# Letting a second query chunk attend while keys and values are still being projected

## The chip, the cores and the metric

The kernel runs on one core of a Trainium2 chip. The metric is the device time of one execution in microseconds. Executions of one kernel agree within about 0.4%.

The engines are named as in the profile: PE (matrix multiplies), PEld (its weight loads), DVE (vector), ACT (activations: exponentials), POOL, and SP, whose queue issues every data transfer. PSUM is the memory that PE writes to.

## The reference, cut to what matters

Two layers, each made of a linear-attention block A and a softmax-attention block B, over S = 2048 positions, D = 1024 features, 32 heads of 32.

```python
def _B_ref(x, wqkv, wo):                       # A is similar, with a feature map in place of softmax
    q, k, v = split_heads(x @ wqkv)            # [H, S, 32] each
    scores = jnp.einsum("bhqd,bhkd->bhqk", q, k) * (Dh ** -0.5)
    p = _softmax(scores, axis=-1)
    o = jnp.einsum("bhqk,bhkd->bhqd", p, v)
    return merge_heads(o) @ wo

for A, B in two layers:                        # shortened
    x = x + _A_ref(_layernorm(x))
    x = x + _B_ref(_layernorm(x))
```

## The kernel before

Positions are cut into four chunks of 512. For each chunk, `to_b(c)` finishes block A, applies the layernorm and projects the keys and values of block B. These projections are the *background*: groups of eight 128x512 matmuls, each of which ends in one PSUM bank that DVE empties.

Attention is cut into *steps*. A step covers four heads (one of 8 head groups g), 256 queries (one of 2 halves) and two key tiles of 128: scores on PE, two exponentials of 128x1024 on ACT, then values and denominators on PE, summed in the PSUM tile ND. A chunk needs 8 x 2 x 8 = 128 steps; a layer has 512, and so 1024 exponentials.

A softmax without the maximum taken off can be summed over key tiles in any order. Chunk 0 therefore attends early: to the keys of chunk c-1 while chunk c is projected. Its partial sums, numerators and denominators, are kept in SBUF.

```python
LAYOUT = {"wide": (0, 8), "mid": (2, 3), "narrow": (3, 1)}   # PSUM: score tiles, background banks

def together(att, blocks, bg, per):            # one step, then `per` units of background work
    bg = iter(bg)
    for b in blocks:
        for _ in b:                            # issues the scores and exponentials of a step
            got = 0.0
            while got < per:                   # a matmul group yields (4, False) and (4, True)
                u, end = next(bg, (1e9, True))
                got += u
                if end:
                    break
            if len(att.lag) > 1:
                att.finish()                   # values and denominators of the step before
    while att.lag:
        att.finish()
    drain(bg)                                  # what is left runs without attention

# in finish(), when a half has seen all key tiles of the block:
    ndc = T("nd", [P, C], F32)
    # ... ndc = nd (+ acc) ...
    rc = T("rc", [P, QH], F32)
    DVE.reciprocal(out=rc[:], in_=ndc[:, QH:C])
    DVE.tensor_tensor(out=oT[...], in0=ndc[:, 0:QH], in1=rc[:], op=ALU.mult)

# one layer
drain(to_b(0, x))
set_mode("mid")
for c in range(1, NCH):
    together(att, [att.block(qs[0], 4 * c - 4, 4 * c, acc, None, c == 1, False)], to_b(c, x), 8)
set_mode("narrow")
for i in range(NCH):                           # chunk 0's last block, then chunks 1, 2, 3 whole
    # ... work: queries of chunk i+1, then after(i-1): output projection and the next layer's keys
    together(att, [block], chain(*work), 8 if i == 0 else 4)
set_mode("wide")
drain(after(NCH - 1, oT, layer, True))
```

Of the kernel before, what the change touches and what calls it, by code (L numbers as in the profile page):

```python
# [9 lines left out]
ALU = mybir.AluOpType  # L10
AX = mybir.AxisListType
ENG = mybir.EngineType
BF16 = mybir.dt.bfloat16
F32 = mybir.dt.float32
# [18 lines left out]
def kernel(  # L33
# [14 lines left out]
    def ppf(w):  # L48
# [4 lines left out]
    serial = [0]  # L53

    BUFS = dict(
        w=3, c8=3, x=2, q=2, kv=2, st=2, E=6, ea=8, acc=4, f=6, r=3, sq=4, nd=2,
        rc=2, kvm=2, sm=6, rcol=3, nc=3, ab=1, t16=1,
    )

    def T(tag, shape, dt):  # L60
        serial[0] += 1
        return sb.tile(shape, dt, tag=tag, name=f"{tag}_{serial[0]}", bufs=BUFS.get(tag, 1))

    def Dr(name, shape, dt=BF16):
        return dram.tile(shape, dt, tag=name, name=name)
# [18 lines left out]
    xb_d = [Dr(f"xb_d{c}", [P, G, C]) for c in range(NCH)]  # L84
    ra_d = [Dr(f"ra_d{c}", [P, C], F32) for c in range(NCH)]
    rb_d = [Dr(f"rb_d{c}", [P, C], F32) for c in range(NCH)]
    kT_d = Dr("kT_d", [P, G, S])
    v_d = Dr("v_d", [P, G, S // P, P])
    wpq_d = Dr("wpq_d", [P, G, D])
# [386 lines left out]
    class Attention:  # L476
# [1 line left out]
            self.lag = []  # L478
            self.nd = None

        def load_kv(self, k0, k1, g):
            kt = T("kv", [P, 2, S], BF16)
            n = k1 - k0
            SP.dma_start(out=kt[:, 0, 0:n * P], in_=kT_d[:, g, k0 * P:k1 * P])
            SP.dma_start(
                out=kt[:, 1, 0:n * P].rearrange("p (t d) -> p t d", d=P),
                in_=v_d[:, g, k0:k1, :],
            )
            return kt

        def block(self, q, k0, k1, acc, oT, first, last):

            kv = self.load_kv(k0, k1, 0)
            for g in range(G):
                nxt = None
                for half in range(2):
                    for kc in range(0, k1 - k0, 2):
                        self.step(q, kv, g, half, kc, kc == 0, kc + 2 == k1 - k0,
                                  acc, oT, first, last)
                        if nxt is None and g + 1 < G:  # L500
                            nxt = self.load_kv(k0, k1, g + 1)
                        yield
                kv = nxt

        def step(self, q, kv, g, half, kc, begin, end, acc, oT, first, last):
            es, tiles = [], []
            for i in range(2):
                tiles.append(ps_tile(f"S{PS['sring'] % PS['ns']}", 2 * C))
                PS["sring"] += 1
            for k in range(2):  # L510
                for j in range(4):
                    rows = slice(32 * j, 32 * j + 32)
                    o = (j % 2) * C + k * QH
                    PE.matmul(  # L514
                        tiles[j // 2][:, o:o + QH],
                        lhsT=kv[rows, 0, (kc + k) * P:(kc + k + 1) * P],
                        rhs=q[rows, g, half * QH:(half + 1) * QH],
                        start=True, stop=True, tile_position=(32 * j, 0),
                        skip_group_check=True,
                    )  # L520
            for i in range(2):
                e = T("E", [P, 2, 2, QH], BF16)
                SC.activation(  # L523
                    out=e[:], in_=tiles[i][:].rearrange("p (j k q) -> p j k q", k=2, q=QH),
                    func=ACT.Exp, scale=SCALE,
                )
                es.append(e)
            self.lag.append((kv, g, half, kc, begin, end, acc, oT, first, last, es))

        def finish(self):  # L530

            kv, g, half, kc, begin, end, acc, oT, first, last, es = self.lag.pop(0)
            if begin:
                self.nd = ps_tile("ND", C)
            nd = self.nd
            for i in range(2):
                for part in range(2):
                    for j in range(4):
                        rows = slice(32 * j, 32 * j + 32)
                        col = (kc + i) * P + 32 * j  # L540
                        PE.matmul(  # L541
                            nd[rows, part * QH:(part + 1) * QH],
                            lhsT=ones_bf[:, 0:32] if part else kv[:, 1, col:col + 32],
                            rhs=es[j // 2][:, j % 2, i, :],
                            start=(begin and i == 0 and part == 0), stop=(end and i == 1),
                            tile_position=(0, 32 * j), skip_group_check=True,
                        )
            if not end:
                return
            if first and not last:  # L550
                DVE.tensor_copy(out=acc[g][:, half, :], in_=nd[:])
                return
            if not first and not last:
                DVE.tensor_tensor(
                    out=acc[g][:, half, :], in0=nd[:], in1=acc[g][:, half, :], op=ALU.add
                )
                return
            ndc = T("nd", [P, C], F32)
            if first:
                DVE.tensor_copy(out=ndc[:], in_=nd[:])  # L560
            else:
                DVE.tensor_tensor(out=ndc[:], in0=nd[:], in1=acc[g][:, half, :], op=ALU.add)  # L562
            rc = T("rc", [P, QH], F32)
            DVE.reciprocal(out=rc[:], in_=ndc[:, QH:C])
            DVE.tensor_tensor(
                out=oT[:, g, half * QH:(half + 1) * QH], in0=ndc[:, 0:QH], in1=rc[:],
                op=ALU.mult,
            )

    def drain(gen):  # L570
        for _ in gen:
            pass

    def together(att, blocks, bg, per):


        bg = iter(bg)
        for b in blocks:
            for _ in b:
                got = 0.0  # L580
                while got < per:
                    u, end = next(bg, (1e9, True))
                    got += u
                    if end:
                        break
                if len(att.lag) > 1:
                    att.finish()
        while att.lag:
            att.finish()
        drain(bg)  # L590
# [19 lines left out]
    def chain(*gens):  # L610
        for g in gens:
            yield from g

    def run():
# [41 lines left out]

        for layer in range(2):
            drain(kv_finish())
            acc = [T(f"acc{g}", [P, 2, C], F32) for g in range(G)]
            x = load_x(0)  # L660

            def to_b(c, x):
                res = {}
                sl = Slabs(["pq", "ao", "bk", "bv"] + (["bq"] if c == 0 else []))
                yield from aq_gen(c, x, sl, res)
                yield from bkv_gen(c, res, sl)
                if c == 0:
                    qs[0] = T("q", [P, G, C], BF16)
                    yield from bq_gen(qs[0], res["xc"], res["rstd"], sl)
                else:  # L670
                    SP.dma_start(out=xb_d[c][:], in_=res["xc"][:])
                    SP.dma_start(out=rb_d[c][:], in_=res["rstd"][:])

            qs = {}
            drain(to_b(0, x))
            set_mode("mid")
            oT = None
            for c in range(1, NCH):
                x = load_x(c)
                together(  # L680
                    att, [att.block(qs[0], 4 * c - 4, 4 * c, acc, None, c == 1, False)],
                    to_b(c, x), 8,
                )
            set_mode("narrow")
            oT = T("c8", [P, G, C], BF16)
            for i in range(NCH):
                work = []
                if i + 1 < NCH:
                    qs[i + 1] = T("q", [P, G, C], BF16)
                    work.append(next_q(i + 1, qs[i + 1]))  # L690
                if i:
                    prev = oT
                    oT = T("c8", [P, G, C], BF16)
                    work.append(after(i - 1, prev, layer))
                block = (
                    att.block(qs[i], 0, S // P, None, oT, True, True) if i
                    else att.block(qs[0], 12, 16, acc, oT, False, True)
                )
                together(att, [block], chain(*work), 8 if i == 0 else 4)
            set_mode("wide")  # L700
            drain(after(NCH - 1, oT, layer, True))


    def setup():
# [21 lines left out]
                    in_=i4[:, s, 4 * g:4 * g + 4].unsqueeze(2).to_broadcast([P, 4, DH]),  # L726
                )

    phi = const("phi", [P, G, P])

    def fold_phi(base, dst):

# [38 lines left out]
    def load_x(c):  # L771
        x = T("x", [P, G, C], BF16)
        SP.dma_start(out=x[:], in_=x_d[c][:])
        return x
# [45 lines left out]
```

## Time and profile before

| | us |
|---|---|
| time, median of 2 runs | 3168.32 (3166.51 to 3170.12) |
| span of the profiled run | 3168.3 |
| PE busy, ACT busy | 81%, 67% of the span |

The page of the kernel before: busy time of the engines, then PE and ACT in 40 equal slices of the span, each digit the busy share in tenths.

```profile
PE 2578.0 (81%) x30208; PEld 1123.8 (35%) x30208; DVE 1276.4 (40%) x1931; ACT 2129.9 (67%) x2433; POOL 95.7 (3%) x88
## 2 busy tenths in 40 slices
PE   4886977888888788878878787878788878878877
...
ACT  2441353535498998898896217262629999999996
```

No engine is full. ACT swings: in each layer three hills with valleys between them (the 6th to 11th digit and the 25th to 30th), then a plateau at 8 or 9. A hill is a projection stage with its 32 steps, a valley the rest of that stage.

The busy time by windows: the stretch and its length, then busy us (and instructions) of PE, PEld, DVE, ACT and POOL, the granted PE clock, the share of DMA engines busy and GB/s. The first two stretches are the chunk-2 stage with and without attention; the third is chunk 0's last block; the fourth is 59 us of attention alone.

```profile
core 0: us, PE busy (x) PEld busy (x) DVE busy (x) ACT busy (x) POOL busy (x), PEclk, DMA share, GB/s
519.20:611.50 92.30, 71.14 (x854) 27.85 (x854) 40.43 (x57) 69.84 (x80) 0.00 (x0) 0.82 0.20 63
611.50:672.30 60.80, 53.29 (x243) 23.46 (x243) 27.60 (x45) 1.36 (x4) 0.00 (x0) 0.89 0.57 189
826.60:894.90 68.30, 57.01 (x833) 25.60 (x834) 48.40 (x54) 59.62 (x65) 0.34 (x2) 1.00 0.35 114
1105.00:1164.00 59.00, 45.90 (x762) 20.46 (x760) 11.47 (x12) 59.00 (x65) 0.00 (x0) 1.00 0.11 37
```

- **Attention alone:** ACT is busy 59.00 of 59 us, and its steps start 1.83 us apart: bound by ACT.
- **The chunk-2 stage:** 92 us with attention (not ACT bound: 69.84 busy), then 61 us in which ACT has 1.36 us of work. That second stretch is the drain at the end of `together`.

A part of the timeline, in chunk 0's last block (start, length, engine, line, operation; tiles written <- read). It shows one step with a whole background group. Line 514 is scores, 158 a background group.

```profile
start us, us, engine line op out<-in xcount [idle before <-releaser]
...
831.56 0.28 PE L514 MATMUL S_1283_7422<-q_2540,kv_7343 32*128 32x256 bf16 x2
...
831.89 1.90 PE L158 MATMUL BG_1287_7436<-c_1272_7363,w_7367 128*128 128x512 bf16 x8
...
834.27 0.28 PE L514 MATMUL S_1290_7467<-q_2540,kv_7343 32*128 32x256 bf16 x2
...
835.15 1.75 DVE L564 RECIPROCAL rc_7464<-nd_7462 128x256 f32<-128x256 f32 x1
...
837.28 0.68 DVE L472 TENSOR_TENSOR q_7342<-BG_1294_7481,r_7364 128x512 bf16<-128x512 f32 x1
```

From scores to scores (831.56 to 834.27) is 2.71 us, all of it PE: 0.33 scores, 1.83 background, 0.55 values (which follow the group at 833.72). A step with a whole group is PE bound.

Step times in this text are the spacing of the first exponentials of successive steps. A stage is counted from its first exponential to that of the next stage.

### The profile page before, as it was taken

To read this page: it belongs to the slowest core of one execution; us is meant where nothing else is said; L and a number is where in the kernel's file an instruction comes from. 1 tells how busy PE (TensorE), PEld (TensorE's weight loads), DVE (VectorE), ACT (ScalarE), POOL (GpSimd) and SP (SyncE) were. 2 spreads that over 40 slices of the span, in tenths; PEclk is the share of its full clock that TensorE was granted. 3 is DMA by queue.
4 is the path that set the end of the run, shared out by engine and by line. 5 is a ranking of instruction groups with operands and counts; after the bars stand their busy time and mean duration, and the time that the engine had idled before them with its cause. 6 is when DMAs were issued, how large, how long until landed. Compare 5 with 4: busy or idle time off the path is not lost.

```text
span 3168.3 us, 68293 instructions
## 1 busy us (share of the span) xinstructions
PE 2578.0 (81%) x30208; PEld 1123.8 (35%) x30208; DVE 1276.4 (40%) x1931; ACT 2129.9 (67%) x2433; POOL 95.7 (3%) x88
## 2 busy tenths in 40 slices
PE   4886977888888788878878787878788878878877
PEld 2442433333433333333333332323233333333333
DVE  2566344444544423523522744444446312322222
ACT  2441353535498998898896217262629999999996
POOL 0320000000000100100100100000000000000000
PEclk8897978887999998999999897879799999999999
DMA  7553505152523113212212251515162211211110
GB/s 191 182 156 122 168 28 193 47 173 69 175 88 127 61 48 111 81 42 98 81 41 93 74 183 47 187 34 189 31 212 87 86 58 42 91 58 41 55 42 15
DMA packets 235241, 309.61 MB, mean 98 GB/s; under 512 B 43456, under 2 KB 207296, under 8 KB 227264
## 3 DMA queue, kind: packets, MB, share of 16 engines
q1 hardware_dynamic: 234944, 305.24, 29.4%
q8 instruction: 236, 3.87, 0.5%
q14 instruction: 61, 0.50, 0.0%
HBM read 236.52 MB, written 60.29 MB: 94 GB/s over the span
## 4 chain that ended last, share of the span: by engine, by line
PE 47%; ACT 28%; DVE 14%; issue 6%; DMA 3%; SPq 1%; ACTq 0%; DVEq 0%; POOLq 0%
SPq L766 1%; DMA v_d<-st_5681 0%; DMA v_d<-st_24626 0%; DMA v_d<-st_4111 0%; DMA w_506<-wpk_d 0%; DMA w_1992<-wpq_d 0%; DMA w_245<-in_A_wqkv_dram 0%; DMA w_10216<-wpk_d 0%; DMA wpk_d<-st_492 0%; PE ND_14215 L541 0%; SPq L737 0%; DVE c_2904_18189 L175 0%; DVE c_2317_14246 L175 0%; DVE c_3634_22833 L175 0%; DVE c_3907_24490 L175 0%
## 5 line engine op out<-in xcount | busy, mean ns | idle before, releaser
L541 PEld LDWEIGHTS <-ones 128*32 128x32 bf16 x8192 | 275.6, 99 | 5.9
L188 PEld LDWEIGHTS <-ones 128*128 128x128 bf16 x128 | 12.7, 101 | 113.0 <-issue 111.6
L193 ACT ACTIVATE f_2352<-BG_432_2319,eps 128x512 f32<-128x512 f32 x1 | 0.7, 687 | 52.1 <-PE BG_432_2319 L188 52.1
L193 ACT ACTIVATE f_22867<-BG_3635_22834,eps 128x512 f32<-128x512 f32 x1 | 0.7, 687 | 50.7 <-PE BG_3635_22834 L188 50.7
L403 PEld LDWEIGHTS <-Rsel 128*128 128x128 bf16 x128 | 13.2, 103 | 59.4 <-issue 58.2
L523 ACT ACTIVATE E_23157<-S_3685_23147 128x1024 bf16<-128x1024 f32 x1 | 1.0, 1026 | 46.1 <-PE S_3686_23148 L514 46.1
L523 ACT ACTIVATE E_2642<-S_482_2632 128x1024 bf16<-128x1024 f32 x1 | 1.0, 1024 | 46.0 <-PE S_483_2633 L514 46.0
L158 PEld LDWEIGHTS <-c_5_187 128*128 128x128 bf16 x128 | 13.4, 106 | 43.3 <-DMA w_506<-wpk_d 22.3
L523 ACT ACTIVATE E_27871<-S_4470_27861 128x1024 bf16<-128x1024 f32 x1 | 1.0, 1024 | 33.5 <-PE S_4471_27862 L514 33.5
L523 ACT ACTIVATE E_7356<-S_1267_7346 128x1024 bf16<-128x1024 f32 x1 | 1.0, 1024 | 33.0 <-PE S_1268_7347 L514 33.0
L523 ACT ACTIVATE E_24727<-S_3946_24717 128x1024 bf16<-128x1024 f32 x1 | 1.0, 1024 | 32.7 <-PE S_3947_24718 L514 32.7
L523 ACT ACTIVATE E_26297<-S_4207_26287 128x1024 bf16<-128x1024 f32 x1 | 1.0, 1024 | 32.5 <-PE S_4208_26288 L514 32.5
L523 ACT ACTIVATE E_5782<-S_1004_5772 128x1024 bf16<-128x1024 f32 x1 | 1.0, 1025 | 31.9 <-PE S_1005_5773 L514 31.9
L523 ACT ACTIVATE E_4212<-S_743_4202 128x1024 bf16<-128x1024 f32 x1 | 1.0, 1025 | 31.4 <-PE S_744_4203 L514 31.4
L158 PE MATMUL BG_77_510<-w_506,c_5_187 128*128 128x512 bf16 x8 | 3.3, 592 | 22.0 <-DMA w_506<-wpk_d 22.0
L158 PEld LDWEIGHTS <-ones 128*128 128x128 bf16 x128 | 12.1, 98 | 24.6 <-issue 10.8
L193 ACT ACTIVATE f_24524<-BG_3908_24491,eps 128x512 f32<-128x512 f32 x1 | 0.7, 687 | 29.1 <-PE BG_3908_24491 L188 29.1
L242 POOL MEMSET acc_1680_9926<- 128x16 bf16 x1 | 0.2, 168 | 631.0 <-DVE nd_7851 L562 631.0
L193 ACT ACTIVATE f_27664<-BG_4430_27631,eps 128x512 f32<-128x512 f32 x1 | 0.7, 687 | 27.5 <-PE BG_4430_27631 L188 27.5
L193 ACT ACTIVATE f_4009<-BG_705_3976,eps 128x512 f32<-128x512 f32 x1 | 0.7, 687 | 27.5 <-PE BG_705_3976 L188 27.5
L193 ACT ACTIVATE f_5579<-BG_966_5546,eps 128x512 f32<-128x512 f32 x1 | 0.7, 687 | 27.5 <-PE BG_966_5546 L188 27.5
L193 ACT ACTIVATE f_7149<-BG_1227_7116,eps 128x512 f32<-128x512 f32 x1 | 0.7, 687 | 27.5 <-PE BG_1227_7116 L188 27.5
(12148 smaller groups left out, 9593.7 us busy)
## 6 DMA issues: line engine op xcount, KB each, us to landing
w_245<-in_A_wqkv_dram SPq DMA_DIRECT2D x1, 1024.0 KB, 5.4
w_247<-in_A_wqkv_dram SPq DMA_DIRECT2D x1, 1024.0 KB, 8.5
xa_d_73<-c_5_187 SPq DMA_DIRECT2D x1, 1024.0 KB, 10.3
x_d_69<-x_167 SPq DMA_DIRECT2D x1, 1024.0 KB, 4.4
x_d_70<-x_234 SPq DMA_DIRECT2D x1, 1024.0 KB, 6.5
xa_d_74<-c_37_346 SPq DMA_DIRECT2D x1, 1024.0 KB, 4.2
x_d_71<-x_704 SPq DMA_DIRECT2D x1, 1024.0 KB, 4.7
x_d_72<-x_1090 SPq DMA_DIRECT2D x1, 1024.0 KB, 5.4
```

Source lines behind the costliest of these rows:

```text
L158: PE.matmul(ps, lhsT=lhsT(po), rhs=rhs(po), start=(po == 0), stop=(po == G - 1))
L188: PE.matmul(ps, lhsT=ones_bf[:], rhs=sq[:], start=(po == 0), stop=(po == G - 1))
L193: SC.activation(out=lnv[:], in_=ps, func=ACT.Ln, scale=1.0 / D, bias=eps_t[:])
L242: POOL.memset(v[:, :, :, P:P + 1], 1.0)
L403: PE.matmul(ps, lhsT=Rsel[:, g, s, :], rhs=ab[:], start=True, stop=True)
L523: SC.activation(out=e[:], in_=tiles[i][:].rearrange("p (j k q) -> p j k q", k=2, q=QH), func=ACT.Exp, scale=SCALE,)
L541: PE.matmul(nd[rows, part * QH:(part + 1) * QH], lhsT=ones_bf[:, 0:32] if part else kv[:, 1, col:col + 32], rhs=es[j // 2][:, j % 2, i, :] ...
L766: SP.dma_start_transpose(out=x[:, po, :], in_=A_x[0, c * C:(c + 1) * C, po * P:(po + 1) * P])
```

## The change

The intent is to give ACT work in the valleys. Chunk 1 attends early too: to keys 0 to 1023 during the chunk-2 stage, and to the next 512 during the chunk-3 stage. Both stages move to the narrow layout (three score tiles, one background bank). Room for a second set of partial sums is made by keeping only numerators in SBUF. Denominators, which are equal in the 32 rows of a head, go to DRAM as one row a head, and come back by a broadcast load. The pacing rule in `together` changes as well: in the middle layout a step may now take two group ends, so two of the short broadcast items.

The core of the diff (the rest passes the new arguments along, lets `load_x` run inside `to_b`, and finds room: five `f` tiles instead of six, `phi` in a shared buffer):

```diff
+    den_d = [Dr(f"den_d{i}", [G, 4, 2, QH], F32) for i in range(2)]
@@ load(), called for the next head group
+            dn = T("dn", [P, 2, QH], F32)
+            for j in range(4):
+                SP.dma_start(
+                    out=dn[32 * j:32 * j + 32, :, :],
+                    in_=den_d[acc[1]][g:g + 1, j, :, :].to_broadcast([DH, 2, QH]),
+                )
@@ finish(), block not the last
+                    DVE.tensor_tensor(out=a, in0=num, in1=a, op=ALU.add)
+                    DVE.tensor_tensor(
+                        out=dt[:, half, :], in0=den, in1=dn[:, half, :], op=ALU.add
+                    )
+                if half == 1:
+                    for j in range(4):
+                        SP.dma_start(
+                            out=den_d[acc[1]][g:g + 1, j, :, :], in_=dt[32 * j:32 * j + 1, :, :]
+                        )
@@ together()
-                while got < per:
+                while got < per and ends < max(1, PS["nb"] - 1):
                     u, end = next(bg, (1e9, True))
                     got += u
-                    if end:
-                        break
+                    ends += end
@@ one layer
             set_mode("mid")
-            # chunk 0 attends to keys of chunk c-1 beside to_b(c), c = 1, 2, 3
+            together(att, [att.block(qs[0], 0, 4, acc[0], None, True, False)], to_b(1), 8)
             set_mode("narrow")
+            together(
+                att,
+                [att.block(qs[0], 4, 8, acc[0], None, False, False),
+                 att.block(qs[1], 0, 8, acc[1], None, True, False)],
+                to_b(2), 8,
+            )
+            together(
+                att,
+                [att.block(qs[0], 8, 12, acc[0], None, False, False),
+                 att.block(qs[1], 8, 12, acc[1], None, False, False)],
+                to_b(3), 8,
+            )
+            together(att, [att.block(qs[0], 12, 16, acc[0], oT[0], False, True)], (), 4)
+            # i = 1: att.block(qs[1], 12, 16, ...) with next_q(2) and after(0), 8 a step, then drained
+            # i = 2, 3: as before
```

(Two comments stand for longer lines.) The tiles `dn` and `dt` have one buffer each.

More of the change, by code (lines that the diff above doesn't have):

```diff
@@ L55 @@
     BUFS = dict(
-        w=3, c8=3, x=2, q=2, kv=2, st=2, E=6, ea=8, acc=4, f=6, r=3, sq=4, nd=2,
+        w=3, c8=3, x=2, q=2, kv=2, st=2, E=6, ea=8, acc=4, f=5, r=3, sq=4, nd=2,
         rc=2, kvm=2, sm=6, rcol=3, nc=3, ab=1, t16=1,
@@ L479, in __init__, with load @@
             self.nd = None
-        def load_kv(self, k0, k1, g):
+        def load(self, k0, k1, g, acc, first):
             kt = T("kv", [P, 2, S], BF16)
@@ L488, in load_kv @@
             )
-            return kt
+            if first:
+                return kt, None
+            dn = T("dn", [P, 2, QH], F32)
[4 more added lines that the diff above has]
+                )
+            return kt, dn
         def block(self, q, k0, k1, acc, oT, first, last):
-            kv = self.load_kv(k0, k1, 0)
+            kv = self.load(k0, k1, 0, acc, first)
             for g in range(G):
@@ L500, in block @@
                         if nxt is None and g + 1 < G:
-                            nxt = self.load_kv(k0, k1, g + 1)
+                            nxt = self.load(k0, k1, g + 1, acc, first)
                         yield
@@ L505, in step @@
         def step(self, q, kv, g, half, kc, begin, end, acc, oT, first, last):
+            kv, dn = kv
             es, tiles = [], []
@@ L527, in step @@
                 es.append(e)
-            self.lag.append((kv, g, half, kc, begin, end, acc, oT, first, last, es))
+            self.lag.append((kv, dn, g, half, kc, begin, end, acc, oT, first, last, es))
         def finish(self):
-            kv, g, half, kc, begin, end, acc, oT, first, last, es = self.lag.pop(0)
+            kv, dn, g, half, kc, begin, end, acc, oT, first, last, es = self.lag.pop(0)
             if begin:
@@ L549, in finish @@
                 return
-            if first and not last:
-                DVE.tensor_copy(out=acc[g][:, half, :], in_=nd[:])
-                return
-            if not first and not last:
-                DVE.tensor_tensor(
-                    out=acc[g][:, half, :], in0=nd[:], in1=acc[g][:, half, :], op=ALU.add
-                )
+            num, den = nd[:, 0:QH], nd[:, QH:C]
+            if not last:
+                a = acc[0][g][:, acc[1], half, :]
+                if half == 0:
+                    self.dt = T("dt", [P, 2, QH], F32)
+                dt = self.dt
+                if first:
+                    DVE.tensor_copy(out=a, in_=num)
+                    DVE.tensor_copy(out=dt[:, half, :], in_=den)
+                else:
+                    DVE.tensor_tensor(out=a, in0=num, in1=a, op=ALU.add)
[7 more added lines that the diff above has]
+                        )
                 return
@@ L561, in finish @@
             else:
-                DVE.tensor_tensor(out=ndc[:], in0=nd[:], in1=acc[g][:, half, :], op=ALU.add)
+                DVE.tensor_tensor(
+                    out=ndc[:, 0:QH], in0=num, in1=acc[0][g][:, acc[1], half, :], op=ALU.add
+                )
+                DVE.tensor_tensor(out=ndc[:, QH:C], in0=den, in1=dn[:, half, :], op=ALU.add)
             rc = T("rc", [P, QH], F32)
@@ L579, in together @@
             for _ in b:
-                got = 0.0
-                while got < per:
+                got, ends = 0.0, 0
+                while got < per and ends < max(1, PS["nb"] - 1):
                     u, end = next(bg, (1e9, True))
                     got += u
-                    if end:
-                        break
+                    ends += end
                 if len(att.lag) > 1:
@@ L658, in run, with to_b @@
             drain(kv_finish())
-            acc = [T(f"acc{g}", [P, 2, C], F32) for g in range(G)]
-            x = load_x(0)
-            def to_b(c, x):
+            tiles = [T(f"acc{g}", [P, 2, 2, QH], F32) for g in range(G)]
+            acc = [(tiles, 0), (tiles, 1)]
+            qs = {}
+            saved = {}
+            def to_b(c):
+                x = load_x(c)
                 res = {}
-                sl = Slabs(["pq", "ao", "bk", "bv"] + (["bq"] if c == 0 else []))
+                sl = Slabs(["pq", "ao", "bk", "bv"] + (["bq"] if c < 2 else []))
                 yield from aq_gen(c, x, sl, res)
                 yield from bkv_gen(c, res, sl)
-                if c == 0:
-                    qs[0] = T("q", [P, G, C], BF16)
-                    yield from bq_gen(qs[0], res["xc"], res["rstd"], sl)
+                if c < 2:
+                    qs[c] = T("q", [P, G, C], BF16)
+                    yield from bq_gen(qs[c], res["xc"], res["rstd"], sl)
                 else:
@@ L672, in to_b @@
                     SP.dma_start(out=rb_d[c][:], in_=res["rstd"][:])
-            qs = {}
-            drain(to_b(0, x))
+            drain(to_b(0))
             set_mode("mid")
-            oT = None
-            for c in range(1, NCH):
-                x = load_x(c)
-                together(
-                    att, [att.block(qs[0], 4 * c - 4, 4 * c, acc, None, c == 1, False)],
-                    to_b(c, x), 8,
-                )
-            set_mode("narrow")
-            oT = T("c8", [P, G, C], BF16)
-            for i in range(NCH):
+            together(att, [att.block(qs[0], 0, 4, acc[0], None, True, False)], to_b(1), 8)
+            set_mode("narrow")
+            together(
[9 more added lines that the diff above has]
+                to_b(3), 8,
+            )
+            oT = [T("c8", [P, G, C], BF16)]
+            together(att, [att.block(qs[0], 12, 16, acc[0], oT[0], False, True)], (), 4)
+            for i in range(1, NCH):
+                oT.append(T("c8", [P, G, C], BF16))
                 work = []
@@ L690, in run @@
                     work.append(next_q(i + 1, qs[i + 1]))
-                if i:
-                    prev = oT
-                    oT = T("c8", [P, G, C], BF16)
-                    work.append(after(i - 1, prev, layer))
+                work.append(after(i - 1, oT[i - 1], layer))
                 block = (
-                    att.block(qs[i], 0, S // P, None, oT, True, True) if i
-                    else att.block(qs[0], 12, 16, acc, oT, False, True)
+                    att.block(qs[i], 0, S // P, None, oT[i], True, True) if i > 1
+                    else att.block(qs[1], 12, 16, acc[1], oT[1], False, True)
                 )
-                together(att, [block], chain(*work), 8 if i == 0 else 4)
+                together(att, [block], chain(*work), 4 if i > 1 else 8)
             set_mode("wide")
-            drain(after(NCH - 1, oT, layer, True))
+            drain(after(NCH - 1, oT[-1], layer, True))
     def setup():
@@ L727, in setup @@
                 )
-    phi = const("phi", [P, G, P])
+    phi = T("t16", [P, G, P], BF16)
     def fold_phi(base, dst):
```

## The prediction

> **What bounds the kernel now.** The span is 3168 us, no engine full: PE busy 81%, ACT 67% (the busy table). Each layer's attention is 512 steps of two 128x1024 exponentials. I cut it into blocks of 32 steps by the exponentials' start times (the view of one source line).
>
> - Attention alone, narrow PSUM layout: 58.9 us a block, 1.83 a step, ACT 40 of 40 us busy (windows): ACT bound.
> - With half a background group (four 128x512 matmuls) a step: 1.85 us, nearly free.
> - With a whole group of eight: 2.71 us, PE bound (timeline: scores 0.33, group 1.83, values 0.55).
> - Projection stages of chunks 1-3 (152.6 us each): 92 us with 32 steps, then 60 us in which ACT idles (windows: 2 of 40 us busy) and PE drains some 30 groups at 1.73 us and a 14 us layernorm. Within the 92 us: query groups 3.0 us a step, an 11.5 us wait for DVE's denominator chain, 22 broadcast steps at 2.4-2.5 us, as the middle layout has two score buffers.
>
> **What the change moves.** No work disappears. Chunk 1's first 12 key tiles (96 of its 128 steps) move under the projections of chunks 2 and 3, in the narrow layout. Estimates from these durations, per layer:
>
> | stage | us |
> |---|---|
> | chunk-1 projection, 32 steps; drained tail gains 8 query groups | 152 |
> | chunk-2 projection, 96 steps: query groups 24, denominator 14, broadcasts 25x1.9=48, whole-group steps 24x2.75=66, layernorm 17, pure steps 60 | 229 |
> | chunk-3 projection, 64 steps | 171 |
> | chunk 0's last block, alone | 59 |
> | chunk 1's last block, whole groups, tail drained | 125 (layer 2: 91) |
> | sum | 736 (702) |
> | now, same work | 797 (768) |
>
> Gain 61 + 66 = 127 us. Two removed drains and faster broadcast steps give some 145 us a layer; overlapped whole groups (+0.9 us each over a pure step), two overlapped layernorms (+10 us each) and chunk 0's results projected under 32, not 128 steps take over half back.
>
> **What it adds.** Per layer 160 broadcast loads and 160 stores of denominators on the SP queue, both tiles single-buffered. Key/value loads take 0.3-0.4 us to issue and at least 2.0 us to land (DMA view), as the Trainium skill has it ("DMA: Bandwidth & Descriptors", Anatomy of one DMA: about 2 us fixed). Per head group: 2+4+4 issues, about 4 us; the store tile is free about 5 us after the sum, wanted after 3.7 in pure steps, 5.4 in whole-group steps; part is hidden. Worse behind 1 MB weight loads (5-6 us). Estimate 10, perhaps 30 us a layer. Two half-width DVE operations for one (0.42 against 0.69): free.
>
> 3168 - 127 + 20 gives about **3065 us**, range **3015 to 3115**. Faster by over 2%: 0.80; within 2%: 0.17; slower: 0.03.
>
> **What would show it.** ACT idle in one drain per layer, after chunk 1's projection; chunk-2 and chunk-3 stages near 230 and 170 us without drained tails; broadcast steps near 1.9 us; whole-group steps near 2.75; DVE waits for denominator transfers of about 1 us, not 3; chunk 1's last stage 125/91 us; later stages unchanged.
>
> **What would make it wrong.** DVE waiting several us a head group on the single denominator buffers, holding the value accumulator and background buffer and so PE; SP delaying weight and key loads; the single background buffer stalling projections.

## The result, and the profile after

The changed kernel took 3075.91 us (2 runs, 3073.64 to 3078.18) against 3168.32 us: ratio 0.9708, 95% interval 0.9667 to 0.975. A ratio here is the mean time of one kernel's runs over that of the other's of the same rounds, so not quite the ratio of the medians. The changed kernel, unedited, ran again as a control (below): 3074.9 us, ratio 0.9699. The forecast of 3065 was 11 us low, inside its range.

The page of the changed kernel, the lines that answer to those of before:

```profile
PE 2471.7 (80%) x29928; PEld 1095.4 (36%) x30208; DVE 1330.2 (43%) x2219; ACT 2136.7 (70%) x2433; POOL 95.7 (3%) x88
## 2 busy tenths in 40 slices
PE   4786879798787778878877787978878887878877
...
ACT  2441263769868558898897306277986877999996
```

PE and ACT do nearly the same work in a shorter span. (Some 280 matmul records are missing from this trace, so its lower PE time says nothing.) ACT's first valley of each layer is still there; the two that followed are mostly filled.

The busy time by windows for layer 1, same columns. In order: chunk-1 stage with attention, its drain; chunk-2 stage with background, its pure steps; chunk-3 stage; chunk 0's last block; chunk 1's last block with attention, its drain.

```profile
368.30:469.10 100.80, 78.10 (x907) 32.05 (x920) 55.60 (x98) 69.39 (x81) 0.00 (x0) 0.91 0.29 98
469.10:516.80 47.70, 46.42 (x237) 22.05 (x242) 18.16 (x28) 1.93 (x3) 0.00 (x0) 0.94 0.59 182
516.80:686.80 170.00, 143.66 (x1801) 61.48 (x1825) 73.92 (x131) 128.75 (x144) 0.00 (x0) 0.92 0.39 127
686.80:748.50 61.70, 48.32 (x806) 21.37 (x807) 6.41 (x18) 60.64 (x67) 0.00 (x0) 1.00 0.17 53
748.50:921.80 173.30, 145.58 (x1841) 62.46 (x1865) 80.48 (x151) 130.57 (x147) 0.00 (x0) 0.91 0.40 127
921.80:983.80 62.00, 46.48 (x766) 20.15 (x767) 44.49 (x61) 59.16 (x64) 0.00 (x0) 0.86 0.32 98
983.80:1095.00 111.20, 87.54 (x959) 37.60 (x973) 74.88 (x114) 64.46 (x71) 3.26 (x4) 0.92 0.44 145
1095.00:1130.10 35.10, 20.24 (x108) 8.69 (x108) 24.45 (x35) 7.55 (x13) 8.95 (x8) 0.62 0.28 90
```

The 61 us drain is gone from the chunk-2 and chunk-3 stages; one of 48 us stays after chunk 1's projection, and there is a new one of 35 us at the end, in which ACT has 7.55 us of work and the granted clock is 0.62.

Stage by stage, us. "Forecast" is the table of the prediction, which left out its 10 us a layer for denominators:

| stage | forecast | layer 1 | layer 2 |
|---|---|---|---|
| chunk-1 projection | 152 | 148.5 | 148.4 |
| chunk-2 projection, 96 steps | 229 | 231.8 | 231.7 |
| chunk-3 projection, 64 steps | 171 | 173.3 | 173.2 |
| chunk 0's last block | 59 | 62.0 | 62.4 |
| chunk 1's last block | 125 / 91 | 146.3 | 97.7 |
| sum | 736 / 702 | 761.9 | 713.4 |
| same work before | 797 / 768 | 798.4 | 772.9 |

The stages give 36.5 + 59.5 = 96.0 us, and the spans differ by 3168.3 - 3071.8 = 96.5: the whole difference lies here. The later stages are as before (chunk 2: 270.2 and 243.0 us against 272.5 and 242.0).

Broadcast steps take 1.81 to 1.84 us in the new chunk-2 stage where nothing waits (mostly 2.39 to 2.5 before), whole-group steps 2.71 to 2.73. The denominators do show. A part of the timeline in that stage (SPq lines are transfers being issued; x4 is four of them; L571 adds denominators, L494 loads them, L576 stores them, L551 is values):

```profile
566.28 0.42 DVE L571 TENSOR_TENSOR dt_5023<-ND_5043,dn_4747 128x256 f32<-128x256 f32 x1
...
566.75 3.04 SPq L494 DMA_DIRECT2D dn_4925<-den_d_89  x4
...
569.83 1.16 SPq L576 DMA_DIRECT2D den_d_89<-dt_5023  x4
...
572.29 0.42 DVE L571 TENSOR_TENSOR dt_5175<-ND_5125,dn_4925 128x256 f32<-128x256 f32 x1 [2.27 <-DMA den_d_89<-dt_5023]
...
572.77 0.29 PE L551 MATMUL ND_5195<-E_5152,kv_4922 128*32 128x256 bf16 x2 [2.19 <-DVE dt_5175 L571]
...
573.82 1.02 ACT L533 ACTIVATE E_5222<-S_915_5212 128x1024 bf16<-128x1024 f32 x1 [1.26 <-PE S_916_5213 L524]
```

The sum in `dt` was ready to be stored at 566.7. SP was then in the four loads of the next `dn`, from 566.75 to 569.8, and got to the stores at 569.83. DVE wanted `dt` again at 570.0 and waited 2.27 us. The label names the stores, but the next sum also reads the `dn` of the four loads: by the semaphore updates in the trace the last load landed at 571.38, the last store at 571.88, so only the last 0.5 us is the stores' alone. PE waited behind DVE, and ACT had nothing to do for 1.26 us. The Trainium skill ("DMA: Bandwidth & Descriptors", Anatomy of one DMA) says that a semaphore wait happens on the issuing sequencer before dispatch. This trace agrees: just before, SP issued nothing from 562.5 to 565.8, where its next load waited for PE. The 3.1 us by which the ready stores were late are issue time in one queue: the four loads took 3.04 us there (one of them 1.50; the trace does not show why), and none of the semaphores that the last three wait for changes in that time. Over the trace there are 45 DVE waits for such transfers, 44 us in all (21 in layer 1, 23 in layer 2).

### The profile page after: what moved, and what is told of

Read it like the earlier page. It is cut to its first block, busy times and chain, and to the rows that moved or that the text cites. A ratio compares the mean times of both kernels' runs of the same rounds, so it can differ in the third digit from the quotient of the medians.

```text
span 3071.8 us, 69543 instructions
## 1 busy us (share of the span) xinstructions
PE 2471.7 (80%) x29928; PEld 1095.4 (36%) x30208; DVE 1330.2 (43%) x2219; ACT 2136.7 (70%) x2433; POOL 95.7 (3%) x88
## 4 chain that ended last, share of the span: by engine, by line
PE 48%; ACT 20%; DVE 18%; DMA 5%; issue 5%; SPq 4%; DVEq 0%; ACTq 0%; POOLq 0%
SPq L494 2%; SPq L797 1%; SPq L576 0%; DVE c_1965_11955 L590 0%; DMA w_12339<-in_B_wo_dram 0%; SPq L486 0%; DMA w_1994<-wpq_d 0%; DMA w_508<-wpk_d 0%; DMA w_33472<-in_B_wo_dram 0%; DMA w_247<-in_A_wqkv_dram 0%; DVE c_5294_33088 L590 0%; SPq L768 0%; DVE c_4036_25094 L176 0%; DVE x_12337 L433 0%; DVE x_33470 L433 0%
## 5 line engine op out<-in xcount | busy, mean ns | idle before, releaser
L551 PEld LDWEIGHTS <-ones 128*32 128x32 bf16 x8192 | 270.3, 99 | 5.4
L159 PEld LDWEIGHTS <-c_6_189 128*128 128x128 bf16 x128 | 13.4, 106 | 42.9 <-DMA w_508<-wpk_d 21.5
L159 PEld LDWEIGHTS <-c_2104_12760 128*128 128x128 bf16 x128 | 13.8, 110 | 33.9 <-issue 26.1
L159 PEld LDWEIGHTS <-ones 128*128 128x128 bf16 x128 | 11.8, 98 | 25.1 <-issue 12.5
L159 PE MATMUL BG_78_512<-w_508,c_6_189 128*128 128x512 bf16 x7 | 3.2, 608 | 21.4 <-DMA w_508<-wpk_d 21.2
L159 PEld LDWEIGHTS <-c_3603_22690 128*128 128x128 bf16 x128 | 12.8, 101 | 15.9 <-issue 1.9
L159 PEld LDWEIGHTS <-c_3031_18809 128*128 128x128 bf16 x128 | 10.5, 98 | 20.6 <-issue 13.3
L159 PEld LDWEIGHTS <-c_205_1204 128*128 128x128 bf16 x128 | 12.5, 98 | 14.6
L159 PEld LDWEIGHTS <-c_2444_14866 128*128 128x128 bf16 x128 | 10.4, 97 | 20.1 <-issue 12.5
L159 PEld LDWEIGHTS <-c_133_818 128*128 128x128 bf16 x128 | 12.4, 98 | 14.4
L159 PEld LDWEIGHTS <-c_38_348 128*128 128x128 bf16 x128 | 12.4, 98 | 14.4
L159 PE MATMUL BG_365_1998<-c_361_1990,w_1994 128*128 128x512 bf16 x7 | 3.4, 630 | 11.5 <-DMA w_1994<-wpq_d 11.3
```

Of the source, the lines that this page charges most:

```text
L159: PE.matmul(ps, lhsT=lhsT(po), rhs=rhs(po), start=(po == 0), stop=(po == G - 1))
L551: PE.matmul(nd[rows, part * QH:(part + 1) * QH], lhsT=ones_bf[:, 0:32] if part else kv[:, 1, col:col + 32], rhs=es[j // 2][:, j % 2, i, :] ...
```

## The experiments

Theory: time falls because attention fills the drains, and this pays only in the narrow layout, where a step without a group takes 1.83 us; the denominators give some 10 us a layer back. Rivals: the layout alone did it; the pacing rule is immaterial; the denominators are free, or all of their waits count.

Runs of one call shared a chip; the medians of the kernel before over the four calls were 3168.2, 3170.3, 3168.6 and 3165.6 us. Intervals are 95%.

### The layout alone, on the kernel before

```diff
-            set_mode("mid")
+            set_mode("narrow")
```

> The kernel before with only the PSUM layout of the three projection stages changed from middle to narrow; nothing moved. Theory (the gain is the moved attention; the layout alone shortens 22 broadcast steps by 0.55 us, -12 us a stage, but costs about 0.9 us for each of 24 drained groups, +22 us): about 8 us a stage slower, 3168 to 3240. Rival (the layout is what made the changed kernel faster): 3080 to 3110.

Measured: 3229.06 us, ratio 1.0191 (1.0176 to 1.0206). Layer 1's three stages took 164.1, 162.8 and 164.7 us against 152.5, 153.1 and 154.3; the time from the last attention step of a stage to the next stage grew from 62 to 64 us to 87 to 89. Broadcast steps did fall to 1.81 us. The rival falls: with nothing moved, the single background bank costs more in the drain than the third score tile gains.

### The moved attention in the old layout

```diff
             together(att, [att.block(qs[0], 0, 4, ...)], to_b(1), 8)
-            set_mode("narrow")
             # chunk-2 and chunk-3 stages
+            set_mode("narrow")
             oT = [T("c8", [P, G, C], BF16)]
```

> The changed kernel with the chunk-2 and chunk-3 stages kept in the middle layout (two score buffers, three background buffers). Theory (moved attention pays only where a pure step takes 1.83 us; in the middle layout some 59 steps a layer without a group take 2.4, part offset by two broadcasts a step): about 37 us a layer slower, 3150 (3130 to 3170). Rival (where attention runs is everything, the layout is immaterial): 3060 to 3090.

Measured: 3188.97 us, ratio 1.0067 (1.0052 to 1.0082), slower than the kernel before, and 114 us above the control's median. The direction is the theory's; the size is not, 57 us a layer instead of 37. Layer 1's chunk-2 stage took 271.5 us against 231.8. Up to its last background group it was shorter, 150.6 against 168.2, as two broadcasts share a step. Then 48 steps without a group took 120.9 us, where the changed kernel has 34 in 63.6. The window of those 48 steps and, from the timeline, one step of them (L524 is scores):

```profile
663.10:784.00 120.90, 94.02 (x1169) 36.87 (x1162) 9.63 (x26) 93.02 (x96) 0.00 (x0) 0.53 0.12 39
```

```profile
699.85 0.61 PE L524 MATMUL S<-q,kv 32*128 32x256 bf16 x6 [0.52 <-ACT E L533]
...
700.36 1.94 ACT L533 ACTIVATE E<-S 128x1024 bf16<-128x1024 f32 x2 [0.56 <-PE S L524]
```

With two score tiles, PE waits for ACT to leave a tile (0.52 us), then ACT waits for PE to fill it (0.56 us): 2.50 us a step, and the granted clock is 0.53. It fell from 1.00 to 0.50 at 669.3; the first two of these steps, before that, took 2.39 us, so most of the loss against 1.83 is there at the full clock. Neither half of the change is worth anything without the other.

### The old pacing rule

```diff
-                while got < per and ends < max(1, PS["nb"] - 1):
+                while got < per and ends < 1:
```

> The changed kernel with the old pacing rule (a step takes background work up to the first end of a group, so one broadcast a step in the middle layout). It acts in the chunk-1 stage alone. Theory (that stage stays at 148 us in spite of 8 more query groups because two broadcasts now share a step, which brings the output projection under attention): that stage goes back to before's 152.6 plus 14 for the query groups, 166 us, so 35 us slower over two layers, about 3111 (3100 to 3120). Rival (the pacing rule is immaterial, the drained tail is hidden either way): 3068 to 3084.

Measured: 3111.31 us, ratio 0.9818 (0.9801 to 0.9836); control below. The chunk-1 stage took 167.5 and 168.1 us, 20 more a layer. So 36 us of the change's gain (3111.3 - 3074.9) hang on this small line: broadcasts take 11 steps instead of 22 or more, and the output projection gets under attention before the steps run out. The other 57 us (3168.3 - 3111.3) are there without it.

One rival stays untested: the line alone in the kernel before. That kernel has three middle-layout stages a layer, whose 32 steps take the same 90 us as in this run's chunk-1 stage. If each gained the 20 us measured here, it would be some 120 us in two layers, more than the whole change. This is an estimate from one stage; no run shows it.

### Control

> The changed kernel itself, unedited, as the yardstick for the other runs on this chip: 3076 within 8 us.

Measured: 3074.9 us, ratio 0.9699 (0.9677 to 0.9721).

### No denominator transfers

Loads and stores are taken out; a constant tile is added instead. The result is wrong on purpose.

```diff
-            dn = T("dn", [P, 2, QH], F32)
-            # four broadcast loads
-            return kt, dn
+            return kt, (None if first else den_c)
@@ finish()
-                if half == 1:
-                    # four stores
```

> Wrong result on purpose: no denominator loads or stores, the partial sums add a constant tile instead; same DVE and PE work. In the trace of the changed kernel DVE waits 21 us in layer 1 and 23 us in layer 2 for these transfers. Theory (part of it reaches the critical path, as predicted 10 us a layer, 12 by the long steps I count): 24 us faster than the changed kernel, about 3052. Rival A (hidden entirely): within 5 us of it, 3071 to 3081. Rival B (every wait counts): 44 us faster, about 3032.

Measured: 3057.14 us, ratio 0.9648 (0.9626 to 0.967), below the control's interval. By medians 18 us, by ratios (the runs are of different calls) 16: 8 or 9 a layer, less than half of the 44 us that DVE waits. In the traces of this run and the changed kernel, the chunk-2 and chunk-3 stages and chunk 0's last block are shorter by 4.9, 2.7 and 2.1 us in layer 1, and 1.9, 2.3 and 1.8 in layer 2. Both rivals fall.

### Loads alone taken out, and two outgoing tiles

First, two tiles for outgoing denominators; the buffers fill SBUF, so one `f` tile goes.

```diff
-        nd=2, f=5,   # shortened
+        nd=2, f=4, dt=2,
```

> The changed kernel with two tiles for outgoing denominators (room made by four instead of five f tiles of the same size). In the control's trace 20 of 28 DVE waits for denominator transfers in layer 1 end with a store. Theory (the single outgoing tile is most of the 19 us that the transfers cost): 8 to 14 us faster, about 3064; chunk-2 and chunk-3 stages 2 to 3 us shorter each. Rival (the waits move to the incoming tile, also single, behind the same SP queue): within 4 us of 3075.

Second, the loads alone out, the stores kept; the result is wrong.

```diff
-            dn = T("dn", [P, 2, QH], F32)
-            # four broadcast loads
-            return kt, dn
+            return kt, (None if first else den_c)
```

> Wrong result on purpose: the denominators are stored as in the changed kernel but not loaded back; a constant tile is added instead, as in the run without any denominator transfers (3057, ratio to before 0.9648). Theory (the loads, behind which the SP queue holds the stores, carry most of the 19 us; two outgoing tiles gave only 4): about as fast as the run without any transfer, ratio 0.964 to 0.966, 3055 to 3061. Rival (the stores carry it): ratio 0.968 to 0.970, 3067 to 3075.

Measured: with two tiles, 3070.59 us, ratio 0.9694 (0.9681 to 0.9708), not to be told from the control; the 8 to 14 us did not come. In its trace DVE still waits 16.1 and 21.9 us a layer for these transfers (control 21.9 and 25.1). The count in the expectation was wrong, too: the control's trace has 20 such waits in layer 1, 12 labelled as stores and 8 as loads; in the changed kernel's first trace 10 of 22 are labelled as loads. The label names only what came last, so it was no ground to choose the tile by: a sum waits for the loads of `dn` as well, and in the step shown above they landed 0.5 us before the stores. That is about all that a second outgoing tile could save there. With the loads gone, 3060.70 us, ratio 0.9669 (0.9654 to 0.9684): by the ratio between the two expectations, by the time at the end of the theory's. Of the ratio's 0.0051 between control and no transfers, the loads carry 0.0030 by the mean values, but the interval overlaps both, so the share is rough. How the rest splits between stores, the SP queue and the short `f` ring stays open.

### Half a group a step in the chunk-2 stage

```diff
-                to_b(2), 8,
+                to_b(2), 4,
```

> The changed kernel with half a background group a step in the chunk-2 stage, whose 96 steps then hold all of its background work by my count of the generator's yields (96), in place of 63 steps with whole groups and 33 pure ones. Theory (a whole-group step is PE bound at 2.71 us, a half-group step is ACT bound at 1.85 as in the trace of before): 24 groups x 0.85 us = 20 us a layer faster, about 3036 (3020 to 3050). Rival (that stage is held by denominator transfers and DVE, not by how groups are spread): within 10 us of 3076.

Measured: 3028.54 us, ratio 0.956 (0.9545 to 0.9576). The stage took 207.6 and 208.6 us, 24 and 23 less. Its window in layer 1:

```profile
514.80:722.40 207.60, 179.59 (x2633) 73.99 (x2632) 81.48 (x149) 187.08 (x211) 0.00 (x0) 0.94 0.35 114
```

ACT is busy 187 of 208 us; the steps with half a group take 1.85 to 1.87 us, as read in the trace of before. Whole groups and pure steps side by side were the waste: 2.71 + 1.83 = 4.54 us for a pair that can take 3.70.

### The reciprocal moved to ACT

```diff
-            DVE.reciprocal(out=rc[:], in_=ndc[:, QH:C])
+            SC.activation(out=rc[:], in_=ndc[:, QH:C], func=ACT.Ln)
+            SC.activation(out=rc[:], in_=rc[:], func=ACT.Exp, scale=-1.0)
```

This asks why every second step of chunk 1's last block takes 3.47 us. The changed kernel's timeline there (L159 is a background group, L433 empties its bank, L589 the reciprocal):

```profile
1011.81 1.90 PE L159 MATMUL BG_2043_12389<-c_1772_10818,w_12339 128*128 128x512 bf16 x8
...
1012.43 1.75 DVE L589 RECIPROCAL rc_12372<-nd_12369 128x256 f32<-128x256 f32 x1
...
1014.56 0.68 DVE L433 TENSOR_TENSOR x_12337<-BG_2043_12389,x_12337 128x512 bf16<-128x512 f32 x1
...
1015.29 1.02 PE L159 MATMUL BG_2049_12430<-c_1772_10818,w_12339 128*128 128x512 bf16 x3 [0.70 <-DVE x_12337 L433]
```

The group is done at 1013.7, but DVE is in the reciprocal and the product and empties the bank at 1014.56; the next group starts at 1015.29 after 0.70 us of waiting.

> The changed kernel with the reciprocal of the denominators moved from DVE (1.75 us, 128x256) to ACT as exp(-ln x), two activations of an estimated 0.5 us each. Theory (in chunk 1's last stage every second whole-group step takes 3.47 instead of 2.71 us because the reciprocal delays the background eviction on DVE): these steps fall to about 2.75, the stage is 10 to 12 us shorter a layer; in chunk 2's and 3's stages the ACT time added (1 us an end, 16 ends each) about cancels what the steps of 3.4 us gain. 3050 to 3080 in all; the stage time decides. Rival (these long steps come from the accumulator or the denominator loads): the 3.47 us steps stay.

Measured: 3107.57 us, ratio 0.9807 (0.9789 to 0.9824): worse as a whole. By the expectation the stage time decides, and it fell from the control's 147.6 to 135.7 us in layer 1; a pair of steps fell from 6.18 (3.47 + 2.71) to 5.48 (3.67 + 1.81). In layer 2 it fell by 2.5 us only. So the reciprocal is the cause of the long steps. The guess that the added ACT time cancels in chunk 2's stage held in layer 1 (269.9 us against the control's 270.4) and not in layer 2 (250.7 against 242.0), and it left out chunk 0's last block: where ACT is the bound, two activations of 0.42 us are paid in full (77.2 us against 64.0).

### The drained tail carried on

With the half groups above. `together` returns what is left instead of draining it, and chunk 2's stage takes it first.

```diff
+        if carry:
+            return bg
         while att.lag:
             att.finish()
@@ i = 1, 2, 3
-                work = []
+                work = [rest]
-                together(att, [block], chain(*work), 4 if i > 1 else 8)
+                rest = together(att, [block], chain(*work), 4 if i > 1 else 8, i == 1) or ()
```

> The changed kernel with half a group a step in the chunk-2 stage (measured alone before: 47 us faster) and with chunk 1's last stage not drained: what is left of its background work is carried into chunk 2's stage, which had over 50 pure steps. Theory (chunk 1's last stage took 146 and 98 us, not my 125 and 91, mostly because the drained tail with one background buffer took 35 us, not 22): the stage falls to about 112 and 83 us, chunk 2's stage grows by 10 and 3 us; together with the half groups 3076 - 47 - 36 = about 2993 (2980 to 3010). Rival (the carried work costs in chunk 2's stage what the drain cost): 3020 to 3035.

Measured: 2998.31 us, ratio 0.9461 (0.9444 to 0.9478). Chunk 1's last block took 118.4 and 83.6 us, chunk 2's stage 281.2 and 242.7 (with half groups alone: 147.0 and 97.9, then 269.9 and 243.0). The tail was idle time for the most part: 29 us went and 11 came back in layer 1; 14 went and none came back in layer 2. Two lines of PE in the drain of the changed kernel show why it was slow:

```profile
1101.75 2.76 PE L159 MATMUL BG_2234_13499<-w_13275,c_2104_12760 128*128 128x512 bf16 x6 [0.22 <-issue]
1108.13 3.57 PE L159 MATMUL BG_2239_13519<-w_13275,c_2104_12760 128*128 128x512 bf16 x8 [3.62 <-DVE f_13509 L219]
```

Within that drain PE waits 3.62 us for DVE to empty the one background bank, and the group then takes 3.57 us instead of 1.90.

### Both, and half groups in chunk 1's last block

```diff
-                together(att, [block], chain(*work), 4 if i > 1 else 8)
+                rest = together(att, [block], chain(*work), 4, i == 1) or ()
```

> Half a group a step in the chunk-2 stage and in chunk 1's last stage too, whose rest is carried into chunk 2's stage. Theory (pairs of steps there fall from 6.18 us, two whole groups, to about 5.2 with one; the moved groups are nearly free in chunk 2's over 40 pure steps): chunk 1's last stage about 84 and 78 us (118 and 84 with whole groups), chunk 2's about 300 and 250 (281 and 243): about 20 us faster than 2998, 2978 (2965 to 2992). Rival (chunk 2's stage gives back all that is taken): 2993 to 3005.

The same with the two tiles for outgoing denominators of above:

> Both of the other two edits of this call: the gains add, about 2968 by the theories; 2978 if only the half groups work.

Measured: 2980.99 us, ratio 0.9415 (0.9402 to 0.9428), chunk 1's last block 81.9 and 82.1 us, chunk 2's stage 303.3 and 244.0. With the second outgoing tile 2972.38 us, ratio 0.9387 (0.9373 to 0.9402), correct. Its 8.6 us over the first are at the edge of the intervals. This is the fastest version found: 6.1% under the kernel before, about 3% under the changed one.

## Why the prediction was right or wrong

- **What bounds the kernel:** right. Steps of 1.83, 1.85 and 2.71 us were found again in the new stages and in the experiments.
- **The gain from filling two drains in the narrow layout:** right in size, 229 and 171 us forecast, 231.8 and 173.3 measured (226.9 and 170.6 without denominators, which the forecast left out of these terms), and shown by two runs to need both the move (ratio 1.0191 without) and the layout (1.0067 without).
- **The chunk-1 stage at 152 us:** 148.5, close. It rested on the pacing rule, which the text did not name; without it 167.5. Whether the 152 was reasoned or lucky cannot be told from the text.
- **Denominators, "10, perhaps 30 us a layer":** right; 8 or 9 a layer. The mechanism was named (single buffers, the SP queue), and the waits are about 1 us as said (44 us / 45), the longest 2.27 us. Its "about 5 us after the sum" came out too: the step shown has the last store land 5.2 us after it. That the stores stand behind the next loads, and that the sum waits for those loads nearly as long, was not said.
- **The step that was off:** the term "chunk 1's last block, whole groups, tail drained, 125 (layer 2: 91)" of the sum. It measured 146.3 and 97.7 us. Two sizes were missed in layer 1. At the end of each half in a last block the reciprocal holds the background bank, so every second whole-group step takes 3.47 instead of 2.71 us. The drain took 35 us, with PE waiting on the one bank and at a clock of 0.62 (read in the trace, not tested apart). Moving the reciprocal takes 12 us off this stage, carrying the tail 29 (17 after what came back).
- **The sum:** a gain of 127 us was forecast before denominators, 96 came. The 31 us between: this term +28 (21 + 7); the chunk-2, chunk-3 and chunk-0 stages +16, where the denominators show; the chunk-1 stage -7; and the stages of before were 6 us longer than summed. The allowance of 20 covered two thirds of it, in part by luck: it was meant for the denominators alone.

## What to carry to other kernels

When two kinds of work share the engines, price each *pairing* from the trace, not each kind: here a step with half a group costs 1.85 us, one with a whole group 2.71 and one with none 1.83, so spreading evenly beats doing it fast and then waiting. A buffer layout is good for one mix of work: moving work and changing the layout each lost time alone and gained together. Count the tail of each overlapped stage, and let what is left run on under the next stage instead of draining it.

## What the Trainium skill lacked or had wrong

- "TensorE: Matmul & The Clock Gate", Part 1, has the half clock come after at least one idle window of about 3.4 us. In the run with the old layout the granted clock was 0.5 for 116 us on end, while no gap between PE records was over 0.63 us; the same matmuls a step in 1.83 us instead of 2.50 kept it at 1.00. PE's busy share does not part the two either: 23.8 of 30 us (672.9 to 702.9 of that run) and 39.6 of 50 us (690 to 740 of the changed kernel), 79% in both. What does is not shown.
- "DMA: Bandwidth & Descriptors" says that semaphore waits are the issuing sequencer's, but not what the order of one queue costs small transfers: four ready stores left 3.1 us late behind four loads. A broadcast load of 32 rows took SP 0.42 us to issue (median of 320), the longest 1.74.
- "ScalarE: Activation LUTs", What it computes, sends reciprocals to the vector engine, and no page that I read gives the time: 1.75 us for 128x256 in fp32 on DVE, against 0.42 us for a product of that size and 0.42 us for each of the two activations that replaced it.
